# A sum over u moved from identity matmuls on TensorE to fp32 adds on VectorE, and its two PSUM banks given to the pools

## The chip, the cores and the metric

The kernel runs on one core of one Trainium2 chip. The metric is device time in microseconds of one execution, median of several runs; runs marked slow by the harness are left out of every comparison. In the profile PE is TensorE's matmuls, PEld its weight loads, DVE is VectorE, ACT is ScalarE, POOL is GpSimd, SP is the queue that issues loads. The matmuls of this kernel write their results to PSUM, of which its pools hold eight banks; a bank is free again when another engine has read the result out (an "eviction", where it is copied).

## The reference, cut to what matters

It is the forward and backward pass of a speech joint network: two strided convolutions with GELU, then a joint `tanh(fe + ge)` over T=4000 frames and U=8 labels, times `w_o`. The part that the change touches is the gradient of `fe`, which is a sum over the eight labels:

```python
fe = jnp.einsum("btd,de->bte", f, w_f)                 # (2, 4000, 256)
ge = jnp.einsum("bud,de->bue", g, w_g)                 # (2, 8, 256)
j = jnp.tanh(fe[:, :, None, :] + ge[:, None, :, :])    # (2, 4000, 8, 256)
return jnp.einsum("btud,dv->btuv", j, w_o)
# backward of this part, written out:
#   gj   = grad_out @ w_o.T
#   gz   = (1 - j*j) * gj            # per u
#   d_fe = sum over u of gz          # the sum of the title
#   d_ge = sum over t of gz
```

## The kernel before: the parts that matter

The frames are cut into 18 chunks (numbered from 0), nine per batch element: one of 256 frames, seven of 512 and one of 160. The main loop runs three stages side by side, each for another chunk: `stage_a(k+1)` (convolutions, GELU and its derivative), `stage_j(k)` (the joint part, 16 steps) and `stage_de(k-1)` (all remaining gradients). Every step of `stage_j` makes one tile NGZ (the negated gz, one u and one half dt of the 256 features). NGZ goes to a PSUM bank of its own through a matmul with the identity, which adds it to what the bank holds:

```python
    gxp = ctx.enter_context(tc.tile_pool(name="gxp", bufs=2))
    psG = ...bufs=1   # the running gradient of w_o
    psS = ...bufs=1   # sum0, sum1: two banks for the sum over u
    psJ = ...bufs=3   # psj: gj, outputs, transposes of JT
    psA = ...bufs=2   # psa: everything of stage_a and stage_de
    # [...]
    def emit_sum(g_, u, dt, NGZ):
        if u == 0:
            S.setdefault("sum", {})[dt] = psS.tile([P, CW], FP32, name=f"sum{dt}")
        ps = S["sum"][dt]
        nc.tensor.matmul(ps[:, :W], lhsT=ident[:], rhs=NGZ[:, :W], start=(u == 0), stop=(u == U - 1))
        if u == U - 1:
            # [...]
            evac(S["NGFE"][:, dt, :W], ps[:, :W], "act" if dt == 0 else "dve")
    # [...] one step of stage_j: u, dt
                gj = ps_j()
                for kt in range(KT):
                    nc.tensor.matmul(gj[:, :W], lhsT=WOT[:, kt, dt * P:(dt + 1) * P], rhs=GOT[:, j, kt, :W], ...)
                if dt == 0:
                    JSQ = jzp.tile([P, KT, CW], BF16, name="JSQ", bufs=2)
                    nc.vector.tensor_tensor(out=JSQ[:, :, :W], in0=JT[:, j, :, :W], in1=JT[:, j, :, :W], op=ALU.mult)
                NGZ = jzp.tile([P, CW], BF16, name="NGZ")
                nc.vector.scalar_tensor_tensor(out=NGZ[:, :W], in0=JSQ[:, dt, :W], scalar=1.0, in1=gj[:, :W],
                                               op0=ALU.subtract, op1=ALU.mult, accum_out=NGGE_parts[...])
                pend_sum.append((g_, u, dt, NGZ))
                # [...] transposes of JT, their copy JR, the output matmuls, the tanh of the next JT
```

In `stage_a` the product FE is copied from PSUM to SBUF by VectorE in step 7. In `stage_de` each block of the gradient of x is evicted from PSUM as two GX_SB halves, one by ScalarE and one by VectorE, and then stored. GX_SB has two buffers. The tool that builds the kernel chooses the order of the instructions and the waits itself, so an edit can move instructions that it doesn't name.

Of the kernel before, what the change touches and what calls it, by code (L numbers as in the profile page):

```python
# [10 lines left out]
BF16 = mybir.dt.bfloat16  # L11
FP32 = mybir.dt.float32
ALU = mybir.AluOpType
ACT = mybir.ActivationFunctionType
# [7 lines left out]
def kernel(  # L22
# [19 lines left out]
    nc = tc.nc  # L42
    B, T, D = x.shape
    KK = w1.shape[0]
    U = g.shape[1]
# [4 lines left out]
    KT = 2  # L50
    P = 128
# [23 lines left out]
    gop = ctx.enter_context(tc.tile_pool(name="gop", bufs=3))  # L75
    jop = ctx.enter_context(tc.tile_pool(name="jop", bufs=2))
    jrp = ctx.enter_context(tc.tile_pool(name="jrp", bufs=3))
    jzp = ctx.enter_context(tc.tile_pool(name="jzp", bufs=4))
    dep = ctx.enter_context(tc.tile_pool(name="dep", bufs=1))
    dep2 = ctx.enter_context(tc.tile_pool(name="dep2", bufs=2))  # L80
    x5p = ctx.enter_context(tc.tile_pool(name="x5p", bufs=4))
    gxp = ctx.enter_context(tc.tile_pool(name="gxp", bufs=2))
    psG = ctx.enter_context(tc.tile_pool(name="psG", bufs=1, space=bass.MemoryType.PSUM))
    psS = ctx.enter_context(tc.tile_pool(name="psS", bufs=1, space=bass.MemoryType.PSUM))
    psJ = ctx.enter_context(tc.tile_pool(name="psJ", bufs=3, space=bass.MemoryType.PSUM))
    psA = ctx.enter_context(tc.tile_pool(name="psA", bufs=2, space=bass.MemoryType.PSUM))

    def ps_j(dt=FP32):
        return psJ.tile([P, CW if dt == FP32 else 2 * CW], dt, name="psj" if dt == FP32 else "psjb", tag="psj")
# [73 lines left out]
    NGGE_all = accp.tile([P, B, KT, U], FP32, name="NGGE_all")  # L163
    NGGE_parts = accp.tile([P, B, KT, U, NC], FP32, name="NGGE_parts")
    GE = accp.tile([P, B, KT, U], FP32, name="GE")
    GWO_ps = psG.tile([P, KT, V], FP32, name="GWO_ps")

    def make_ge():
# [16 lines left out]
    def evac(out, in_, eng=None):  # L185
        if eng is None:
            eng = "act" if ev_ctr[0] % 2 == 0 else "dve"
            ev_ctr[0] += 1
        if eng == "act":
            nc.scalar.copy(out=out, in_=in_)  # L190
        else:
            nc.vector.tensor_copy(out=out, in_=in_)  # L192
# [50 lines left out]
    def stage_a(g_):  # L243
        b, ci, c0, W = chunks[g_]
        S = st[g_]
        XC = xc_tiles.pop(g_)
        if g_ + 1 < NG:
            xc_tiles[g_ + 1] = load_xc(g_ + 1)
        HTe = htp.tile([P, KT, CW], BF16, name="HTe")
        HTo = htp.tile([P, KT, 2 + CW], BF16, name="HTo")  # L250
        G1e = keep.tile([P, KT, CW], BF16, name="G1e")
        G1o = keep.tile([P, KT, 2 + CW], BF16, name="G1o")
        if ci == 0:
            nc.gpsimd.memset(HTo[:, :, 0:2], 0.0)
            nc.gpsimd.memset(G1o[:, :, 0:2], 0.0)
        else:
            pv = st[g_ - 1]
            pw = chunks[g_ - 1][3]
            nc.gpsimd.tensor_copy(out=HTo[:, :, 1:2], in_=pv["HTo"][:, :, pw + 1:pw + 2])
            nc.gpsimd.tensor_copy(out=G1o[:, :, 1:2], in_=pv["G1o"][:, :, pw + 1:pw + 2])  # L260
        S["HTo"], S["G1e"], S["G1o"] = HTo, G1e, G1o
        mm_o = [(W1[:, i, kt], XC[c][:, kt, 16:16 + W]) for i, c in ((0, 1), (1, 2), (2, 3)) for kt in range(KT)]
        yield from conv_gelu(W, mm_o, HTo[:, :, 2:2 + W], G1o[:, :, 2:2 + W])
        mm_e = [(W1[:, i, kt], XC[c][:, kt, 16 + sh:16 + sh + W])
                for i, c, sh in ((0, 3, -1), (1, 0, 0), (2, 1, 0)) for kt in range(KT)]
        yield from conv_gelu(W, mm_e, HTe[:, :, 0:W], G1e[:, :, 0:W], ps_j if g_ == 0 else None)
        last = c0 + W == MQ
        FT = htp.tile([P, KT, CW], BF16, name="FT")
        G2 = keep.tile([P, KT, CW], BF16, name="G2")
        S["G2"] = G2  # L270
        mm_f = [(W2[:, i, kt], SRC[:, kt, off:off + W])
                for i, SRC, off in ((0, HTo, 1), (2, HTo, 2), (1, HTe, 0)) for kt in range(KT)]
        yield from conv_gelu(W, mm_f, FT[:, :, 0:W], G2[:, :, 0:W])
        S["FE"] = []
        for mt in range(KT):
            ps = ps_a()
            for kt in range(KT):
                nc.tensor.matmul(ps[:, :W], lhsT=WF[:, kt, mt * P:(mt + 1) * P], rhs=FT[:, kt, :W],  # L278
                                 start=(kt == 0), stop=(kt == KT - 1))
            FE = fep.tile([P, CW], FP32, name=f"FE{mt}")  # L280
            evac(FE[:, :W], ps[:, :W], "dve")
            S["FE"].append(FE)
        yield
        HRo = keep.tile([P, NB, D], BF16, name="HRo")
        HRe = keep.tile([P, NB, D], BF16, name="HRe")
        FR = keep.tile([P, NB, D], BF16, name="FR")
        S["HRo"], S["HRe"], S["FR"] = HRo, HRe, FR
        to_rows(HRo, HTo, 1, W + 1 if last else W)
        yield
        to_rows(HRe, HTe, 0, W)  # L290
        yield
        to_rows(FR, FT, 0, W)
        yield
# [20 lines left out]
                                     start=(n == 0), stop=(n == n_gwo - 1))  # L314
                    gwo_cnt[0] = n + 1

    pend_sum, pend_gwo = [], []

    def emit_sum(g_, u, dt, NGZ):
        W = chunks[g_][3]  # L320
        S = st[g_]
        if u == 0:
            S.setdefault("sum", {})[dt] = psS.tile([P, CW], FP32, name=f"sum{dt}")
        ps = S["sum"][dt]
        nc.tensor.matmul(ps[:, :W], lhsT=ident[:], rhs=NGZ[:, :W], start=(u == 0), stop=(u == U - 1))
        if u == U - 1:
            if "NGFE" not in S:
                S["NGFE"] = dep2.tile([P, KT, CW], BF16, name="NGFE")
            evac(S["NGFE"][:, dt, :W], ps[:, :W], "act" if dt == 0 else "dve")

    def stage_j(g_):

# [2 lines left out]
        for up in range(UP):  # L335
# [8 lines left out]
            for step in range(4):  # L344
# [7 lines left out]
                        after(mm, conv_last, sync=False)  # L352
                if dt == 0:
                    JSQ = jzp.tile([P, KT, CW], BF16, name="JSQ", bufs=2)
                    nc.vector.tensor_tensor(out=JSQ[:, :, :W], in0=JT[:, j, :, :W], in1=JT[:, j, :, :W], op=ALU.mult)  # L355
                NGZ = jzp.tile([P, CW], BF16, name="NGZ")
                nc.vector.scalar_tensor_tensor(out=NGZ[:, :W], in0=JSQ[:, dt, :W], scalar=1.0, in1=gj[:, :W],  # L357
                                               op0=ALU.subtract, op1=ALU.mult,
                                               accum_out=NGGE_parts[:, b, dt, u, ci:ci + 1])
                pend_sum.append((g_, u, dt, NGZ))  # L360
                if len(pend_sum) > 2:
                    emit_sum(*pend_sum.pop(0))
                if step % 2 == 0:
                    tbs = [t_ for t_ in nblk[g_] if t_[0] // 2 == step // 2]
                    if tbs:
# [72 lines left out]
    def stage_de(g_):  # L438
# [86 lines left out]
        for bl, m in sblk:  # L525
            GX = gxp.tile([P, 4, D], BF16, name="GX_SB")
            for cp in range(2):
                ps = ps_a()
                for cj in range(2):
                    mms = [(SRC[:, kt, off + bl * P:off + bl * P + m], W1T[:, i, kt, :])  # L530
                           for SRC, off, i in rows4[2 * cp + cj] for kt in range(KT)]
                    for k, (l_, r_) in enumerate(mms):
                        nc.tensor.matmul(ps[:m, cj * D:(cj + 1) * D], lhsT=l_, rhs=r_,  # L533
                                         start=(k == 0), stop=(k == len(mms) - 1))
                evac(GX[:m, 2 * cp:2 * cp + 2].rearrange("p c d -> p (c d)"), ps[:m, :], "act" if cp == 0 else "dve")
                yield
            s0 = c0 + bl * P
            r0, r1 = (1 if s0 == 0 else 0), (m - 1 if s0 + m - 1 == MQ else m)
            dst = out_1[b, 0:1, :]
            flat = GX[:].rearrange("p c d -> p (c d)")  # L540
            if r0 == 1:
                nc.gpsimd.dma_start(out=out_1[b, 0:1, :], in_=GX[0:1, 3, :])
            nc.gpsimd.dma_start(out=bass.AP(tensor=dst.tensor, offset=dst.offset + (4 * (s0 + r0) - 3) * D,
                                            ap=[[4 * D, r1 - r0], [1, 4 * D]]), in_=flat[r0:r1])
            if r1 < m:
                nc.gpsimd.dma_start(out=out_1[b, 4 * MQ - 3:4 * MQ, :].rearrange("(o f) d -> o f d", o=1),
                                    in_=GX[r1:m, 0:3, :])
# [10 lines left out]
    nc.scalar.activation(out=warm_[:, 1, 0:8], in_=warm[:, 0:8], func=ACT.Gelu_apprx_tanh)  # L558
    for _ in range(20):
        nc.tensor.matmul(warm_ps[:, 0:2 * P], lhsT=warm[:, 0:P], rhs=warm, start=True, stop=True)  # L560
    gen = stage_a(0)
    next(gen)
    first_mm, conv_o = marks[0], marks[5]
    nc.sync.dma_start_transpose(out=WOT[:], in_=w_o[:, :])
    st[0]["GOT"], st[0]["GO"] = {0: load_got(0, 0)}, {0: load_gor(0, 0)}
    next(gen)
    next(gen)
    next(gen)
# [57 lines left out]
    for k in range(NG + 1):  # L626
# [14 lines left out]
                for _ in gen:  # L641
                    pass
        if k == NG - 1:
            while pend_sum:
                emit_sum(*pend_sum.pop(0))
            while pend_gwo:
                emit_gwo(*pend_gwo.pop(0))
            gg_out()
            store(out_7, GWO_ps[:])
# [30 lines left out]
```

## Time and profile before

| | before |
|---|---|
| median of 4 runs | 1015.1 us (1007.6 to 1018.6) |
| profiled run | 1005.3 us, clock 0.988 |
| PE, DVE, ACT busy | 966.8, 780.4, 558.6 us |
| a full chunk, mean of ten | 59.96 us |

The "full chunk" is worked out from the trace: the time between NGZ number 16k and number 16(k+1), which is one chunk of `stage_j`, over the ten chunks of 512 frames that have such chunks on both sides as well (k = 2 to 6 and 10 to 14).

The page of the kernel before, its parts 1 and 2 (busy time and share of each engine; then 40 slices of the span, each digit a busy share in tenths):

```profile
span 1005.3 us, 20283 instructions
## 1 busy us (share of the span) xinstructions
PE 966.8 (96%) x8060; PEld 696.6 (69%) x8060; DVE 780.4 (78%) x1733; ACT 558.6 (56%) x983; POOL 211.3 (21%) x402
## 2 busy tenths in 40 slices
PE   5899999999999999999999999999999999999997
...
DVE  3988886959778696868787885958879597877673
ACT  3966674655556464535755664636656455554522
```

TensorE is busy from the second slice to the last but one, and VectorE swings between 5 and 9 with the period of a chunk.

One steady chunk of the kernel before, cut at every fourth NGZ (columns: busy time of each engine with its number of instructions, then clock and DMA):

```profile
core 0: us, PE busy (x) PEld busy (x) DVE busy (x) ACT busy (x) POOL busy (x), PEclk, DMA share, GB/s
162.60:176.20 13.60, 13.50 (x95) 8.19 (x93) 11.05 (x22) 8.45 (x16) 2.82 (x6) 1.00 1.15 210
176.20:192.90 16.70, 16.60 (x132) 10.77 (x130) 16.56 (x36) 10.60 (x17) 1.90 (x4) 1.00 0.80 196
192.90:207.20 14.30, 14.30 (x143) 11.85 (x142) 11.53 (x23) 10.59 (x18) 2.08 (x4) 1.00 0.29 90
207.20:221.70 14.50, 14.45 (x129) 11.66 (x126) 8.71 (x18) 4.67 (x9) 4.65 (x9) 1.00 0.53 162
```

In the second quarter (steps 5 to 8) both PE (16.60 of 16.70 us) and DVE (16.56) look full.

The groups of the kernel before that the change names (busy us, mean ns of one):

```profile
L357 DVE SCALAR_TENSOR_TENSOR NGZ<-JSQ,psj 128x512 bf16<-128x512 bf16 (+2 forms) x288 | 174.2, 611 | 55.3 <-PE psj L349 54.9
L355 DVE TENSOR_TENSOR JSQ<-JT 128x1024 bf16<-128x1024 bf16 (+2 forms) x144 | 87.3, 615 | 2.4
L192 DVE CAST GX_SB<-psa 128x512 bf16<-128x512 f32 x64 | 44.2, 691 | 45.0 <-PE psa L533 33.6
```

The 288 identity matmuls took 58.6 us of TensorE's time from each one's start to the next matmul's start; a full one, 512 columns, takes 216 ns in that sense, although its own record says 379 ns, since matmuls overlap.

The waits of the kernel before that concern GX_SB (total us, times, longest):

```profile
ACT GX_SB L190 <- DMA out_dram<-GX_SB: 37.1, 14, 4.8
DVE GX_SB L192 <- DMA out_dram<-GX_SB: 11.2, 8, 2.3
PE psa L502 <- ACT GX_SB L190: 9.6, 8, 2.2
```

The evictions wait for an older store to leave their buffer, hold their psa bank meanwhile, and TensorE then waits for the bank.

### The profile page before, as it was taken

What the parts mean: (1) busy time and instruction counts of PE and PEld (TensorE: products, weight loads), DVE (VectorE), ACT (ScalarE), POOL (GpSimd) and SP (SyncE); (2) the same over time, 40 slices, a digit from 0 to 9 for tenths busy, and PEclk for the clock granted to TensorE, in tenths of its full rate; (3) what the DMA queues carried; (4) which work ended last, traced back from release to release, by engine and by line L of the source; (5) the groups of instructions that cost most, each with busy time, mean ns of one, the idle gap of its engine ahead of it and who ended that gap; (6) DMA issues with size and microseconds to landing.
All of it is one profiled execution on the core that took longest, in us unless ns stands there. A gap on an engine that the chain in (4) does not pass through costs nothing.

```text
span 1005.3 us, 20283 instructions
## 1 busy us (share of the span) xinstructions
PE 966.8 (96%) x8060; PEld 696.6 (69%) x8060; DVE 780.4 (78%) x1733; ACT 558.6 (56%) x983; POOL 211.3 (21%) x402
## 2 busy tenths in 40 slices
PE   5899999999999999999999999999999999999997
PEld 4567676776767668785765676676867767787873
DVE  3988886959778696868787885958879597877673
ACT  3966674655556464535755664636656455554522
POOL 2122112121111213123231112121121211212230
PEclk7999999999999999999999999999999999999997
DMA  8998848569473774947473847749484684836232
GB/s 168 178 219 207 191 126 180 145 179 196 137 179 107 147 192 148 172 138 197 120 187 103 192 112 179 162 127 220 130 197 110 162 175 130 170 119 168 93 109 61
DMA packets 237919, 156.58 MB, mean 156 GB/s; under 512 B 209504, under 2 KB 213632, under 8 KB 237824
## 3 DMA queue, kind: packets, MB, share of 16 engines
q0 software_dynamic: 29152, 102.69, 34.2%
q1 hardware_dynamic: 206800, 51.68, 31.4%
q8 instruction: 63, 1.03, 0.4%
q10 hardware_dynamic: 1872, 0.92, 0.3%
q14 instruction: 32, 0.26, 0.1%
HBM read 54.44 MB, written 50.34 MB: 104 GB/s over the span
## 4 chain that ended last, share of the span: by engine, by line
PE 80%; ACT 7%; DMA 6%; DVE 5%; SPq 1%; issue 1%; ACTq 0%; DVEq 0%; POOLq 0%
PE psa L502 14%; PE GWO_ps L313 10%; PE psj L387 9%; PE psa L233 9%; PE psj L349 9%; PE psa L533 7%; PE psab L199 6%; PE psjb L371 5%; DMA out_dram<-GX_SB 5%; PE psa L476 3%; ACT JT L300 2%; ACT g_s L216 1%; PE psa L482 1%; DMA GOT<-in_grad_out_dram 1%; ACT OUT_SB L190 1%; PE psa L278 1%
## 5 line engine op out<-in xcount | busy, mean ns | idle before, releaser
L190 ACT CAST OUT_SB<-psj 128x512 bf16<-128x512 f32 (+1 forms) x256 | 150.3, 587 | 165.4 <-PE psj L387 161.2
L357 DVE SCALAR_TENSOR_TENSOR NGZ<-JSQ,psj 128x512 bf16<-128x512 bf16 (+2 forms) x288 | 174.2, 611 | 55.3 <-PE psj L349 54.9
L349 PE MATMUL psj<-GOT,WOT 128*128 128x512 bf16 (+2 forms) x576 | 158.0, 351 | 7.8 <-DMA GOT<-in_grad_out_dram 6.6
L387 PE MATMUL psj<-WO,JT 128*128 128x256 bf16 (+1 forms) x1024 | 162.6, 273 | 0.2
L313 PE MATMUL GWO_ps<-GO_R,JR 128*128 128x256 bf16 (+1 forms) x1024 | 140.6, 273 | 0.0
L210 ACT ACTIVATE g_sq<-psa 128x512 bf16<-128x512 f32 (+2 forms) x106 | 57.7, 544 | 125.1 <-PE psa L233 122.7
L387 PEld LDWEIGHTS <-JT 128*128 128x128 bf16 (+1 forms) x1024 | 93.7, 98 | 38.5 <-issue 3.2
L313 PEld LDWEIGHTS <-JR 128*128 128x128 bf16 (+1 forms) x1024 | 98.5, 98 | 19.2 <-issue 2.3
L129 POOL DMA_DIRECT2D GO_R<-in_grad_out_dram x72 | 52.8, 734 | 268.5 <-PE GWO_ps L313 174.7
L192 DVE COPY JR<-psjb 128x1024 bf16<-128x1024 bf16 (+2 forms) x136 | 88.4, 653 | 10.7 <-PE psjb L371 10.7
L233 PE MATMUL psa<-XC,W_120 128*128 128x512 bf16 (+2 forms) x420 | 92.4, 353 | 1.3 <-DMA XC<-in_x_dram 1.2
L398 POOL DMA_DIRECT2D out_dram<-OUT_SB x72 | 53.4, 742 | 177.8 <-ACT OUT_SB L190 143.3
L355 DVE TENSOR_TENSOR JSQ<-JT 128x1024 bf16<-128x1024 bf16 (+2 forms) x144 | 87.3, 615 | 2.4
L371 PEld LDWEIGHTS <-JT 128*128 128x128 bf16 (+1 forms) x1024 | 69.9, 98 | 27.3 <-issue 0.9
L371 PE MATMUL psjb<-ident,JT 128*128 128x128 bf16 (+1 forms) x1024 | 88.0, 219 | 0.0
L192 DVE CAST GX_SB<-psa 128x512 bf16<-128x512 f32 x64 | 44.2, 691 | 45.0 <-PE psa L533 33.6
L436 DVE TENSOR_TENSOR ACC_GW_148<-ACC_GW_148,psa 128x512 f32<-128x512 f32 x48 | 33.0, 688 | 57.5 <-PE psa L502 57.5
L190 ACT CAST GX_SB<-psa 128x512 bf16<-128x512 f32 x64 | 37.4, 585 | 71.3 <-DMA out_dram<-GX_SB 37.1
L533 PE MATMUL psa<-W1T,GHo 128*128 128x256 bf16 (+1 forms) x384 | 74.1, 275 | 1.2 <-ACT GX_SB L190 1.0
L212 DVE SCALAR_TENSOR_TENSOR g_s<-g_sq,psa 128x512 bf16<-128x512 bf16 (+2 forms) x106 | 65.1, 614 | 12.2 <-ACT HTo L211 11.1
L349 PEld LDWEIGHTS <-WOT 128*128 128x128 bf16 x576 | 54.8, 98 | 28.4 <-DMA WOT<-in_w_o_dram 5.8
L533 PE MATMUL psa<-W1T,GHe 128*128 128x256 bf16 (+1 forms) x384 | 74.0, 275 | 0.1
(616 smaller groups left out, 1886.5 us busy)
## 6 DMA issues: line engine op xcount, KB each, us to landing
GO_R<-in_grad_out_dram POOLq DMA_DIRECT2D x56, 512.0 KB, 4.6
out_dram<-OUT_SB POOLq DMA_DIRECT2D x56, 512.0 KB, 5.4
out_dram<-GX_SB POOLq DMA_DIRECT2D x60, 256.0 KB, 3.2
GOT<-in_grad_out_dram SPq DMA_TRANSPOSE x144, 5.4
GO_R<-in_grad_out_dram POOLq DMA_DIRECT2D x8, 256.0 KB, 4.4
out_dram<-OUT_SB POOLq DMA_DIRECT2D x8, 256.0 KB, 4.5
XC<-in_x_dram SPq DMA_TRANSPOSE x72, 4.7
out_dram<-g_sq SPq DMA_DIRECT2D x9, 128.0 KB, 1.9
```

Source lines behind the costliest of these rows:

```text
L190: nc.scalar.copy(out=out, in_=in_)
L192: nc.vector.tensor_copy(out=out, in_=in_)
L212: nc.vector.scalar_tensor_tensor(out=th, in0=sq, scalar=1.0, in1=ps, op0=ALU.add, op1=ALU.mult)
L233: mm = nc.tensor.matmul(ps[:, :W], lhsT=w[:, mt * P:(mt + 1) * P], rhs=rhs, start=(k == 0), stop=(k == len(mms) - 1))
L313: nc.tensor.matmul(GWO_ps[:, dt, :], lhsT=JR[:m, tb % 2, j, dt * P:(dt + 1) * P], rhs=GO[:m, tb, j, :], start=(n == 0), stop=(n == n_gwo - 1))
L349: mm = nc.tensor.matmul(gj[:, :W], lhsT=WOT[:, kt, dt * P:(dt + 1) * P], rhs=GOT[:, j, kt, :W], start=(kt == 0), stop=(kt == KT - 1))
L355: nc.vector.tensor_tensor(out=JSQ[:, :, :W], in0=JT[:, j, :, :W], in1=JT[:, j, :, :W], op=ALU.mult)
L357: nc.vector.scalar_tensor_tensor(out=NGZ[:, :W], in0=JSQ[:, dt, :W], scalar=1.0, in1=gj[:, :W], op0=ALU.subtract, op1=ALU.mult, accum_out= ...
L371: nc.tensor.transpose(out=tr[:m, o:o + P], in_=JT[:, jj, kt, tb * P:tb * P + m], identity=ident[:])
L387: nc.tensor.matmul(ps[:m, jj * V:(jj + 1) * V], lhsT=JT[:, jj, kt, tb * P:tb * P + m], rhs=WO[:, kt, :], start=(kt == 0), stop=(kt == KT - 1))
L502: nc.tensor.matmul(ps[:, dt * D:(dt + 1) * D], lhsT=lhs(bl, m, dt), rhs=rhs[:m, bl, :], start=(k == 0), stop=(k == n - 1))
L533: nc.tensor.matmul(ps[:m, cj * D:(cj + 1) * D], lhsT=l_, rhs=r_, start=(k == 0), stop=(k == len(mms) - 1))
```

## The change

Its intent: take the identity matmuls off TensorE, pay for the sum with adds on VectorE, and pay for those adds by moving squares and fp32 copies from VectorE to ScalarE. The two banks of the sum go to psj (3 to 4) and psa (2 to 3), and GX_SB gets a third buffer, for which the tiles HRo, HRe and FR (rows of the forward results, kept for the gradients) give up one of three. The core of the diff:

```diff
+    keep2 = ctx.enter_context(tc.tile_pool(name="keep2", bufs=2))        # HRo, HRe, FR (were 3)
-    gxp = ctx.enter_context(tc.tile_pool(name="gxp", bufs=2))
+    gxp = ctx.enter_context(tc.tile_pool(name="gxp", bufs=3))
-    psS = ctx.enter_context(tc.tile_pool(name="psS", bufs=1, ...PSUM))
-    psJ = ctx.enter_context(tc.tile_pool(name="psJ", bufs=3, ...PSUM))
-    psA = ctx.enter_context(tc.tile_pool(name="psA", bufs=2, ...PSUM))
+    psJ = ctx.enter_context(tc.tile_pool(name="psJ", bufs=4, ...PSUM))
+    psA = ctx.enter_context(tc.tile_pool(name="psA", bufs=3, ...PSUM))
+    ZS = accp.tile([P, KT, CW], FP32, name="ZS")
-            evac(FE[:, :W], ps[:, :W], "dve")
+            evac(FE[:, :W], ps[:, :W], "act")
-                    nc.vector.tensor_tensor(out=JSQ[...], in0=JT[...], in1=JT[...], op=ALU.mult)
+                    nc.scalar.activation(out=JSQ[...], in_=JT[...], func=ACT.Square)
-                NGZ = jzp.tile([P, CW], BF16, name="NGZ")
+                first, fin_ = u == 0, u == U - 1
+                NGZ = ZS[:, dt] if first else jzp.tile([P, CW], FP32, name="NGZ", bufs=2)
                 nc.vector.scalar_tensor_tensor(out=NGZ[:, :W], ...)
-                pend_sum.append((g_, u, dt, NGZ))          # -> identity matmul
+                if not first:
+                    nc.vector.tensor_tensor(out=S["NGFE"][:, dt, :W] if fin_ else ZS[:, dt, :W],
+                                            in0=ZS[:, dt, :W], in1=NGZ[:, :W], op=ALU.add)
-                evac(GX[...], ps[:m, :], "act" if cp == 0 else "dve")
+                evac(GX[...], ps[:m, :], "act")
 # [...] at the start, the loads of WOT and of the first GOT and GO are issued before those of the second chunk's x
```

More of the change, by code (lines that the diff above doesn't have):

```diff
@@ L81 @@
     x5p = ctx.enter_context(tc.tile_pool(name="x5p", bufs=4))
-    gxp = ctx.enter_context(tc.tile_pool(name="gxp", bufs=2))
+    gxp = ctx.enter_context(tc.tile_pool(name="gxp", bufs=3))
     psG = ctx.enter_context(tc.tile_pool(name="psG", bufs=1, space=bass.MemoryType.PSUM))
-    psS = ctx.enter_context(tc.tile_pool(name="psS", bufs=1, space=bass.MemoryType.PSUM))
-    psJ = ctx.enter_context(tc.tile_pool(name="psJ", bufs=3, space=bass.MemoryType.PSUM))
-    psA = ctx.enter_context(tc.tile_pool(name="psA", bufs=2, space=bass.MemoryType.PSUM))
+    psJ = ctx.enter_context(tc.tile_pool(name="psJ", bufs=4, space=bass.MemoryType.PSUM))
+    psA = ctx.enter_context(tc.tile_pool(name="psA", bufs=3, space=bass.MemoryType.PSUM))
     def ps_j(dt=FP32):
@@ L280, in stage_a @@
             FE = fep.tile([P, CW], FP32, name=f"FE{mt}")
-            evac(FE[:, :W], ps[:, :W], "dve")
+            evac(FE[:, :W], ps[:, :W], "act")
             S["FE"].append(FE)
         yield
-        HRo = keep.tile([P, NB, D], BF16, name="HRo")
-        HRe = keep.tile([P, NB, D], BF16, name="HRe")
-        FR = keep.tile([P, NB, D], BF16, name="FR")
+        HRo = keep2.tile([P, NB, D], BF16, name="HRo")
+        HRe = keep2.tile([P, NB, D], BF16, name="HRe")
+        FR = keep2.tile([P, NB, D], BF16, name="FR")
         S["HRo"], S["HRe"], S["FR"] = HRo, HRe, FR
@@ L315, in emit_gwo @@
                     gwo_cnt[0] = n + 1
-    pend_sum, pend_gwo = [], []
-    def emit_sum(g_, u, dt, NGZ):
-        W = chunks[g_][3]
-        S = st[g_]
-        if u == 0:
-            S.setdefault("sum", {})[dt] = psS.tile([P, CW], FP32, name=f"sum{dt}")
-        ps = S["sum"][dt]
-        nc.tensor.matmul(ps[:, :W], lhsT=ident[:], rhs=NGZ[:, :W], start=(u == 0), stop=(u == U - 1))
-        if u == U - 1:
-            if "NGFE" not in S:
-                S["NGFE"] = dep2.tile([P, KT, CW], BF16, name="NGFE")
-            evac(S["NGFE"][:, dt, :W], ps[:, :W], "act" if dt == 0 else "dve")
+    pend_gwo = []
     def stage_j(g_):
@@ L354, in stage_j @@
                     JSQ = jzp.tile([P, KT, CW], BF16, name="JSQ", bufs=2)
-                    nc.vector.tensor_tensor(out=JSQ[:, :, :W], in0=JT[:, j, :, :W], in1=JT[:, j, :, :W], op=ALU.mult)
-                NGZ = jzp.tile([P, CW], BF16, name="NGZ")
+                    if True:
+                        nc.scalar.activation(out=JSQ[:, :, :W], in_=JT[:, j, :, :W], func=ACT.Square)
+                    else:
+                        nc.vector.tensor_tensor(out=JSQ[:, :, :W], in0=JT[:, j, :, :W], in1=JT[:, j, :, :W],
+                                                op=ALU.mult)
+                first, fin_ = u == 0, u == U - 1
+                NGZ = ZS[:, dt] if first else jzp.tile([P, CW], FP32, name="NGZ", bufs=2)
                 nc.vector.scalar_tensor_tensor(out=NGZ[:, :W], in0=JSQ[:, dt, :W], scalar=1.0, in1=gj[:, :W],
@@ L359, in stage_j @@
                                                accum_out=NGGE_parts[:, b, dt, u, ci:ci + 1])
-                pend_sum.append((g_, u, dt, NGZ))
-                if len(pend_sum) > 2:
-                    emit_sum(*pend_sum.pop(0))
+                if fin_ and dt == 0:
+                    S["NGFE"] = dep2.tile([P, KT, CW], BF16, name="NGFE")
+                if not first:
+                    nc.vector.tensor_tensor(out=S["NGFE"][:, dt, :W] if fin_ else ZS[:, dt, :W], in0=ZS[:, dt, :W],
+                                            in1=NGZ[:, :W], op=ALU.add)
                 if step % 2 == 0:
@@ L534, in stage_de @@
                                          start=(k == 0), stop=(k == len(mms) - 1))
-                evac(GX[:m, 2 * cp:2 * cp + 2].rearrange("p c d -> p (c d)"), ps[:m, :], "act" if cp == 0 else "dve")
+                evac(GX[:m, 2 * cp:2 * cp + 2].rearrange("p c d -> p (c d)"), ps[:m, :], "act")
                 yield
@@ L560 @@
         nc.tensor.matmul(warm_ps[:, 0:2 * P], lhsT=warm[:, 0:P], rhs=warm, start=True, stop=True)
+    nc.sync.dma_start_transpose(out=WOT[:], in_=w_o[:, :])
+    st[0]["GOT"], st[0]["GO"] = {0: load_got(0, 0)}, {0: load_gor(0, 0)}
     gen = stage_a(0)
@@ L563 @@
     first_mm, conv_o = marks[0], marks[5]
-    nc.sync.dma_start_transpose(out=WOT[:], in_=w_o[:, :])
-    st[0]["GOT"], st[0]["GO"] = {0: load_got(0, 0)}, {0: load_gor(0, 0)}
     next(gen)
@@ L643 @@
         if k == NG - 1:
-            while pend_sum:
-                emit_sum(*pend_sum.pop(0))
             while pend_gwo:
```

## The prediction

> **What bounds the kernel now.** TensorE. The page gives PE busy 966.8 of 1005.3 us (96%) at clock 0.988, and the chain that ended last is 80% PE. "Busy" flatters it: costing the 8060 matmuls at the trace's back-to-back starts (216 ns for 512 columns, 109 for 256) they need about 916 us (an estimate); 84 us are waits, start and tail. DVE is busy 780 us (78%), ACT 559 (56%). Averages hide stages. Cutting a steady chunk (59 to 61 us, 16 steps) at every fourth NGZ operation of the instruction records, at start-to-start costs: steps 1-4 13.6 us, PE 0.98, DVE 0.78, ACT 0.58; steps 5-8 16.7 us, PE 0.96, **DVE 0.99**, ACT 0.60; steps 9-12 14.3 us, PE 0.97, DVE 0.76, ACT 0.69; steps 13-16 14.2 to 16.5 us, PE down to 0.86, DVE 0.5, ACT 0.26. The last varies as GX_SB waits for its older store (37 us in the list of waits; 4.6% of the chain).
>
> **Removed.** 288 identity matmuls: 58.6 us of PE. On DVE: 144 squares JSQ (686 ns, 600 start to start; 76 us), 36 FE copies (19 us), 64 GX casts (38 us), half the NGFE evictions (5 us).
>
> **Added.** DVE: 252 fp32 adds. The Trainium skill ("VectorE: DVE Perf Modes", tier table and errata section) keeps fp32 tensor_tensor in 1x and gives (N+151)/0.96 = 691 ns at N=512. The trace's fp32 accumulator adds (one PSUM operand) agree: 686 to 688 ns, 600 start to start. So 196 x 0.60 plus the narrow ones = 133 us: DVE comes out level in sum, plus bubbles: JSQ and the NGZ that reads it now start 744 ns apart, not 600; an add reads what was just written, so where nothing is interleaved it costs 0.14 us more: 10 to 20 us. ACT: 144 squares (its 128x1024 tanh takes 1067 ns, 957 start to start: 121 us), FE (15), GX (30): ACT rises to about 75% busy.
>
> **On the critical path.** PE work per full chunk falls 16 x 0.216 = 3.5 us. In steps 5-8 DVE stays at 16.5 us (lost: 2 squares, 2 FE copies; gained: 4 adds), so DVE sets that quarter, and steps 1-4 rise to DVE 11.8 of 12.8 us: the first half of the chunk gains about 1 us of its 1.7. Steps 9-12 gain nearly 0.9 us, with ACT near 0.93. Steps 13-16 gain 0.9, and the third GX_SB buffer and third psa bank should take away most GX store waits (10 to 15 us in all). WOT and the first GOT loaded ahead of the second chunk's x shorten the 5.8 us wait for GOT at the start by 2 to 4 us. Two HRo/HRe/FR buffers instead of three make their evictions wait for the older chunk's weight-gradient matmuls: 0 to 8 us. Sum: -55 us.
>
> **Predicted: 957 us**, 935 to 985 (8 in 10). Faster by over 2%: 0.87; within 2%: 0.11; slower: 0.02.
>
> **What would show it.** 7772 matmuls, PE busy near 910 us; DVE within 20 us of 780; ACT near 740; adds near 690 ns, NGZ near 680; GX_SB's store waits mostly gone; steps 5-8 near 16 us with DVE at 0.98 or more; new waits of gj matmuls (psj) for NGZ, or of NGZ for the ACT square.
>
> **What would make it wrong.** Adds dearer than 600 ns; ACT's in-order queue delaying squares, NGZ and its PSUM bank; the two-buffer row tiles blocking; the instruction order changing more than the diff shows; DMA (66% share now) stalling a faster kernel.

## The result, and the profile after

| | before | after |
|---|---|---|
| median | 1015.1 us | 949.5 us |
| fast runs | 1007.6 to 1018.6 (4) | 945.5 to 950.2 (3) |
| profiled run | 1005.3 us | 947.0 us |
| full chunk, mean of ten | 59.96 us | 56.27 us |

The ratio is 0.935, with a 95% interval of 0.927 to 0.943: faster. A fourth run after, of 974 us, was marked slow. Ratios here are the mean time of one kernel's fast runs over the mean of the other's fast runs in the same rounds, so they are not quite the ratio of the medians quoted beside them.

The page of the changed kernel, parts 1 and 2:

```profile
span 947.0 us, 19927 instructions
## 1 busy us (share of the span) xinstructions
PE 911.3 (96%) x7772; PEld 670.1 (71%) x7772; DVE 756.0 (80%) x1723; ACT 710.1 (75%) x1209; POOL 212.7 (22%) x402
## 2 busy tenths in 40 slices
PE   7888999999999999999999999999999999999997
...
DVE  4969895978869697877778796978969687887673
ACT  5979887777968778675878787787878779685642
```

PE has 288 matmuls fewer and is busy 55.5 us less, DVE is about level, ACT has 151.5 us more. PE's share is 96% as before.

A steady chunk of the changed kernel, cut in the same way:

```profile
158.70:174.40 15.70, 15.36 (x112) 9.47 (x110) 12.53 (x26) 13.66 (x22) 3.29 (x7) 1.00 1.11 260
174.40:191.10 16.70, 16.41 (x142) 11.68 (x141) 16.70 (x35) 12.96 (x22) 2.18 (x4) 1.00 0.67 140
191.10:201.70 10.60, 10.18 (x105) 8.50 (x103) 8.70 (x19) 9.60 (x16) 2.07 (x3) 1.00 0.35 100
201.70:215.00 13.30, 13.30 (x126) 11.24 (x124) 8.45 (x17) 7.58 (x14) 4.16 (x8) 1.00 0.55 172
```

The second quarter still lasts 16.70 us with DVE at 16.70 (near 16 us was predicted); but the third lost 3.7 us, and the first gained 2.1. The whole chunk is shorter by 3.7 us.

The groups of the changed kernel that answer to those of before:

```profile
L351 DVE SCALAR_TENSOR_TENSOR NGZ<-JSQ,psj 128x512 f32<-128x512 bf16 (+2 forms) x252 | 152.1, 609 | 53.6 <-PE psj L338 33.5
L345 ACT ACTIVATE JSQ<-JT 128x1024 bf16<-128x1024 bf16 (+2 forms) x144 | 137.7, 956 | 16.5 <-DVE NGZ L351 16.0
L357 DVE TENSOR_TENSOR ZS<-ZS,NGZ 128x512 f32<-128x512 f32 (+2 forms) x216 | 132.1, 612 | 1.3
L191 ACT CAST GX_SB<-psa 128x512 bf16<-128x512 f32 (+1 forms) x128 | 73.3, 591 | 4.8 <-PE psa L529 4.2
```

An fp32 result makes NGZ no dearer (the full ones last 679 ns, 681 before). A full add lasts 683 ns (mean) and the next operation starts 602 ns after it (median). The bubble that the prediction feared (an add that reads what was just written starts late) is there, but rare: of the 252 adds 52 stand directly behind the NGZ that they read, 42 of them full ones, and these start 0.71 to 0.73 us after it, where an operation that doesn't read NGZ starts 0.61 us after it (median). That makes about 5 us in all (an estimate from these counts); before the other adds at least one more operation is interleaved. No wait of GX_SB for its own store appears in the list of waits any more.

Where the 58.3 us between the two profiled runs lie, by the same cuts (us of the span):

| stretch | before | after | difference |
|---|---|---|---|
| to the first NGZ | 25.3 | 21.3 | -4.0 |
| chunks 0 and 1 | 78.5 | 81.3 | +2.8 |
| ten full chunks | 599.6 | 562.7 | -36.9 |
| the other six chunks and the tail | 301.9 | 281.7 | -20.2 |

The first NGZ comes 4.0 us earlier, and the next two chunks give 2.8 us of that back.

### The profile page after: what moved, and what is told of

Same layout as the page of the kernel before. It is cut to its first block, busy times and chain, and to the rows that moved or that the text cites. A ratio compares the mean times of both kernels' runs of the same rounds, so it can differ in the third digit from the quotient of the medians.

```text
span 947.0 us, 19927 instructions
## 1 busy us (share of the span) xinstructions
PE 911.3 (96%) x7772; PEld 670.1 (71%) x7772; DVE 756.0 (80%) x1723; ACT 710.1 (75%) x1209; POOL 212.7 (22%) x402
## 3 DMA queue, kind: packets, MB, share of 16 engines
q0 software_dynamic: 29152, 102.69, 36.9%
## 4 chain that ended last, share of the span: by engine, by line
PE 57%; ACT 27%; DVE 10%; DMA 2%; SPq 2%; issue 2%; DVEq 0%; ACTq 0%
PE psa L498 12%; PE psa L529 9%; ACT JT L301 8%; PE psj L383 8%; PE psj L338 6%; PE GWO_ps L314 6%; ACT JSQ L345 5%; PE psa L234 5%; PE psjb L367 4%; ACT OUT_SB L191 3%; PE psab L200 3%; PE psa L472 3%; ACT g_sq L211 2%; DVE g_s L213 2%; DVE GF L463 2%
## 5 line engine op out<-in xcount | busy, mean ns | idle before, releaser
L351 DVE SCALAR_TENSOR_TENSOR NGZ<-JSQ,psj 128x512 f32<-128x512 bf16 (+2 forms) x252 | 152.1, 609 | 53.6 <-PE psj L338 33.5
L301 ACT ACTIVATE JT<-FE,GE 128x512 bf16<-128x512 f32 (+2 forms) x288 | 183.0, 684 | 0.0
L383 PE MATMUL psj<-WO,JT 128*128 128x256 bf16 (+1 forms) x1024 | 157.5, 274 | 1.3 <-DVE JR L193 1.3
L345 ACT ACTIVATE JSQ<-JT 128x1024 bf16<-128x1024 bf16 (+2 forms) x144 | 137.7, 956 | 16.5 <-DVE NGZ L351 16.0
L357 DVE TENSOR_TENSOR ZS<-ZS,NGZ 128x512 f32<-128x512 f32 (+2 forms) x216 | 132.1, 612 | 1.3
L432 DVE TENSOR_TENSOR ACC_GW<-ACC_GW,psa 128x512 f32<-128x512 f32 x96 | 65.3, 683 | 60.5 <-PE psa L498 60.5
L234 PEld LDWEIGHTS <-W 128*128 128x128 bf16 x648 | 61.9, 98 | 47.1 <-issue 4.6
L234 PE MATMUL psa<-XC,W 128*128 128x512 bf16 (+2 forms) x420 | 92.7, 353 | 1.3 <-DMA XC<-in_x_dram 0.7
L498 PEld LDWEIGHTS <-X 128*128 128x128 bf16 (+1 forms) x768 | 75.0, 98 | 14.0 <-issue 0.6
L191 ACT CAST GX_SB<-psa 128x512 bf16<-128x512 f32 (+1 forms) x128 | 73.3, 591 | 4.8 <-PE psa L529 4.2
```

The lines of the kernel that those rows point to most:

```text
L191: nc.scalar.copy(out=out, in_=in_)
L234: mm = nc.tensor.matmul(ps[:, :W], lhsT=w[:, mt * P:(mt + 1) * P], rhs=rhs, start=(k == 0), stop=(k == len(mms) - 1))
L301: nc.scalar.activation(out=JT[:, j, mt, :W], in_=st[g_]["FE"][mt][:, :W], func=ACT.Tanh, bias=GE[:, b, mt, 2 * up + j:2 * up + j + 1], sca ...
L345: nc.scalar.activation(out=JSQ[:, :, :W], in_=JT[:, j, :, :W], func=ACT.Square)
L357: nc.vector.tensor_tensor(out=S["NGFE"][:, dt, :W] if fin_ else ZS[:, dt, :W], in0=ZS[:, dt, :W], in1=NGZ[:, :W], op=ALU.add)
L383: nc.tensor.matmul(ps[:m, jj * V:(jj + 1) * V], lhsT=JT[:, jj, kt, tb * P:tb * P + m], rhs=WO[:, kt, :], start=(kt == 0), stop=(kt == KT - 1))
```

## The experiments

Two readings stood against each other. The first, that of the prediction: TensorE's removed work is the gain, and VectorE caps it, since VectorE sets the pace of steps 5 to 8. The second: VectorE's fullness there is only a queue running behind, TensorE sets the pace throughout, and what decides is whether TensorE finds free PSUM banks. A third thing to settle was how much each part brings. Each run was timed in three rounds against the kernel before on its chip (medians of before: 1013.0 to 1015.2 us). "Chunk" is the full chunk as above, and "NGZ 33" the time at which chunk 2 begins.

| run | median us | ratio to before | chunk us | NGZ 33 at us |
|---|---|---|---|---|
| before | 1015 | 1 | 59.96 | 103.8 |
| b_gx3 | 1002.3 | 0.991 | 59.31 | 109.1 |
| b_moves | 1019.1 | 1.007 | 60.86 | 108.5 |
| the changed kernel | 949.5 | 0.935 | 56.27 | 102.6 |
| a_fe_dve | 962.9 | 0.947 | 57.10 | 102.6 |
| a_gx_dve | 949.7 | 0.935 | 56.27 | 103.5 |
| a_sq_dve | 959.5 | 0.949 | 56.07 | 113.4 |
| a_bf16 | 944.1 | 0.927 | 55.78 | 105.1 |
| a_noadd (wrong) | 939.7 | 0.926 | 55.98 | 98.3 |
| a_fe_dve_noadd (wrong) | 943.1 | 0.933 | 55.52 | 106.5 |
| a_banks_before | 989.0 | 0.978 | 58.57 | 105.1 |
| a_psa2 | 981.0 | 0.968 | 57.71 | 107.2 |
| a_psj3 | 955.3 | 0.943 | 56.59 | 106.3 |
| a_bf16_psa4 | 933.0 | 0.918 | 55.08 | 103.4 |

The intervals of the ratios are about plus or minus 0.007, some 7 us, and the changed kernel was not timed again beside its variants; so a difference of 5 to 10 us between two variants rests more on the chunk column, where most full chunks of one run agree within 0.1 us. The last column comes from one profiled execution and also depends on when loads land: TensorE's waits for GOT sum to between 1.4 us (a_fe_dve) and 12.1 us (a_sq_dve) over these runs. All results but the two marked ones were correct.

### FE back on VectorE, and half of GX back on VectorE

```diff
 # a_fe_dve
-            evac(FE[:, :W], ps[:, :W], "act")
+            evac(FE[:, :W], ps[:, :W], "dve")
 # a_gx_dve
-                evac(GX[...], ps[:m, :], "act")
+                evac(GX[...], ps[:m, :], "act" if cp == 0 else "dve")
```

> The changed kernel with its 36 FE evictions back on VectorE (19 us of DVE work, all in steps 5-8 of a chunk). Stage theory (VectorE sets the pace of steps 5-8, where it is 1.00 occupied): each full chunk grows by 2 x 0.6 us, so about +12 to +18 us: 961 to 968 us. Rival (TensorE alone sets the pace, VectorE at 80% has room): within 4 us of the changed kernel, 945 to 953 us.

> The changed kernel with half of the GX evictions back on VectorE (64 casts, 38 us of DVE work, twice that of the FE run, but in steps 9-16 where VectorE is 0.8 and 0.6 occupied). Stage theory: within 5 us of the changed kernel (945 to 954 us). If instead VectorE's total counted, it would cost about twice what the FE run costs, 25 us or more.

Measured: FE costs 13 us (962.9 against 949.5) for 19 us of VectorE work; GX costs nothing (949.7) for twice as much. So it matters where in the chunk VectorE's work lies, and not only how much there is. But the two runs don't yet say that VectorE sets the pace of steps 5 to 8. VectorE in the run with FE on VectorE, and then in the changed kernel, around the same place of the same chunk (start, length, line, operation):

```profile
188.40 0.68 DVE L223 TENSOR_TENSOR G<-g_om,g_s 128x1024 bf16<-128x1024 bf16 x1
189.00 1.28 DVE L193 COPY FE<-psa 128x512 f32<-128x512 f32 x2
190.20 0.67 DVE L432 TENSOR_TENSOR ACC_GWF<-ACC_GWF,psa 128x512 f32<-128x512 f32 x1
190.79 0.67 DVE L351 SCALAR_TENSOR_TENSOR NGZ<-JSQ,psj 128x512 f32<-128x512 bf16 x1
```

```profile
187.51 0.68 DVE L223 TENSOR_TENSOR G<-g_om,g_s 128x1024 bf16<-128x1024 bf16 x1
188.11 0.68 DVE L432 TENSOR_TENSOR ACC_GWF<-ACC_GWF,psa 128x512 f32<-128x512 f32 x1
188.71 0.67 DVE L351 SCALAR_TENSOR_TENSOR NGZ<-JSQ,psj 128x512 f32<-128x512 bf16 x1
```

The two FE copies put 1.2 us ahead of two operations that each set a PSUM bank free: the add ACC_GWF a psa bank, the NGZ a psj bank. But TensorE's waits begin earlier, and they point to the banks that the copies themselves hold. The matmuls that made FE, and the next that needs a psa bank, with FE on VectorE (in brackets the idle time before and what ended it):

```profile
184.57 0.59 PE L279 MATMUL psa<-FT,WF 128*128 128x512 bf16 x2
187.20 1.03 PE L498 MATMUL psa<-NFR,FR 128*128 128x256 bf16 x8 [0.71 <-ACT GFR L191]
```

In the changed kernel:

```profile
183.68 0.59 PE L279 MATMUL psa<-FT,WF 128*128 128x512 bf16 x2
184.26 1.08 ACT L191 COPY FE<-psa 128x512 f32<-128x512 f32 x2
185.35 1.04 PE L498 MATMUL psa<-NFR,FR 128*128 128x256 bf16 x8
```

On VectorE the FE copies wait in a queue without a gap, and end 5.3 us after their matmuls (counted from the last matmul's start plus 216 ns; chunks 3 to 6), against 1.2 to 1.4 us on ScalarE. Meanwhile two of the three psa banks are taken. Costed as in "The banks" below, TensorE's waits in steps 5 to 8 rise from 0.79 to 1.74 us, 0.87 us of them before these NFR matmuls, 0.46 us behind VectorE's late copy JR, which frees a psj bank.

### FE on VectorE without the adds

```diff
 # a_fe_dve_noadd: a_fe_dve, and
-                if not first:
+                if fin_:
                     nc.vector.tensor_tensor(out=..., in0=ZS[:, dt, :W], in1=NGZ[:, :W], op=ALU.add)
```

> Wrong on purpose (only the last add of each sum is kept), with the FE evictions on VectorE: the FE run (13 us slower) without the adds. Theory that FE on VectorE costs only because VectorE's queue has a backlog in steps 5-8 there, which delays the evictions behind it: without the adds it costs under 5 us, 937 to 945 us against 939.7 of the run without adds. If FE on VectorE costs by itself, whatever the load: 950 us or more.

Measured: 943.1 us, 3.4 us more than the run without adds and without this edit (939.7, below). So most of the 13 us go when the adds go, as the backlog theory expected: the steady chunk isn't longer with FE on VectorE (55.52 against 55.98 us); what is lost lies before chunk 2 (106.5 against 98.3 us). The trace doesn't show that the queue is empty, though: the FE copies still start 3.1 us or more after their matmuls. Why they then cost nothing in the steady chunk is not shown.

### The adds made cheaper, and left out

```diff
 # a_bf16
-    ZS = accp.tile([P, KT, CW], FP32, name="ZS")
+    ZS = accp.tile([P, KT, CW], BF16, name="ZS")
-                NGZ = ZS[:, dt] if first else jzp.tile([P, CW], FP32, name="NGZ", bufs=2)
+                NGZ = ZS[:, dt] if first else jzp.tile([P, CW], BF16, name="NGZ", bufs=4)
 # a_noadd
-                if not first:
+                if fin_:
```

> The changed kernel with ZS and NGZ in bf16[...]: add 330 ns start to start instead of 600 (414 ns instead of 683 in the record), VectorE busy about 66 us less. Stage theory: steps 5-8 fall from 16.7 to about 15.6 us, whole kernel 8 to 18 us faster, 931 to 941 us. Rival (VectorE not binding): no gain, 945 to 951 us. The gradients are rounded more often, so the comparison with the reference may suffer.

> Wrong on purpose: of the seven adds per sum only the last is kept (216 of 252 adds gone), nothing else changed. This is the upper bound of any cheaper sum. Stage theory: steps 5-8 become bound by TensorE (about 15.3 us), steps 1-4 too; 12 to 30 us faster, 920 to 937 us. Rival (adds lie under TensorE's work): within 4 us of the changed kernel.

Measured: 944.1 and 939.7 us, 5 and 10 us faster than the changed kernel. Both lie between the two ranges, just outside what the prediction's reading expected. (a_bf16 also gives NGZ four buffers instead of two; that was not run apart.) Without six of seven adds the second quarter falls to 15.2 us, but the third rises from 10.6 to 12.7 us, and the chunk falls only from 56.27 to 55.98 us. The largest part of the 9.9 us between the two profiled runs lies before chunk 2, which begins at 98.3 instead of 102.6 us. So the six adds in seven cost about 0.3 us per steady chunk, not the 0.7 us that the prediction withheld.

### Only the moves to ScalarE

```diff
 # b_moves: the kernel before, with
-                    nc.vector.tensor_tensor(out=JSQ[...], in0=JT[...], in1=JT[...], op=ALU.mult)
+                    nc.scalar.activation(out=JSQ[...], in_=JT[...], func=ACT.Square)
-            evac(FE[:, :W], ps[:, :W], "dve")
+            evac(FE[:, :W], ps[:, :W], "act")
-                evac(GX[...], ps[:m, :], "act" if cp == 0 else "dve")
+                evac(GX[...], ps[:m, :], "act")
```

> The kernel before with only the moves to ScalarE (squares, FE, GX evictions); the sum stays on TensorE and the banks and buffers stay as before. VectorE busy falls by about 130 us to 650, ScalarE rises to about 730. My theory: what is worth most is the 58.6 us of TensorE work, so this alone gains little: steps 5-8 fall to TensorE's 16 us, 0 to 15 us faster, 1000 to 1015 us against 1015. Rival (the moves are the gain and VectorE was the bound): 30 us or more faster.

Measured: 1019.1 us, ratio 1.007 (1.000 to 1.014): no gain, if anything a small loss. The page of this run, part 1:

```profile
PE 974.0 (96%) x8060; PEld 697.5 (68%) x8060; DVE 647.4 (63%) x1489; ACT 719.7 (71%) x1227; POOL 212.0 (21%) x402
```

VectorE is relieved of 133 us, and its second quarter does shrink, from 16.7 to 15.1 us; the third grows from 14.3 to 16.8 (columns as above):

```profile
182.00:197.10 15.10, 14.67 (x109) 8.91 (x106) 14.16 (x32) 11.74 (x19) 1.27 (x4) 1.00 0.69 176
197.10:213.90 16.80, 16.55 (x165) 13.57 (x165) 9.09 (x19) 14.57 (x23) 2.69 (x4) 1.00 0.33 97
```

By itself this run leaves a rival: it also loads ScalarE with 161 us, and a new wait there could hide what VectorE's relief gave. TensorE's own records settle it. Costed as in "The banks" below, TensorE waited 0.64 of the 16.7 us of steps 5 to 8 in the kernel before, 0.30 of them directly behind VectorE, and 0.79 of 16.7 us in the changed kernel, 0.16 of them directly behind VectorE (means of chunks 3 to 6). VectorE did not set the pace of steps 5 to 8. The cuts are made at VectorE's own operations. A quarter shows when VectorE gets to an NGZ, and when VectorE is late in one quarter it catches up in the next, while TensorE goes on as long as it has banks. The sum over the chunk is what counts.

### The squares back on VectorE

```diff
 # a_sq_dve
-                        nc.scalar.activation(out=JSQ[...], in_=JT[...], func=ACT.Square)
+                        nc.vector.tensor_tensor(out=JSQ[...], in0=JT[...], in1=JT[...], op=ALU.mult)
```

> The changed kernel with the squares back on VectorE (76 us of work). VectorE would be needed for about 800 us start to start, 0.6 us more in each of 8 pairs of steps; steps 1-8 bound by VectorE at about 31 us instead of 32.3 total as they stand plus 2.4: stage theory +25 to +45 us, 975 to 995 us. If VectorE's average share counted (88% of 950): within 10 us.

Measured: 959.5 us, 10 us slower; the expectation of 25 to 45 us, made on the prediction's reading, was far off. The steady chunk is not longer at all (56.07 us), although its VectorE is busy all through steps 5 to 12. The loss is in the start: chunk 2 begins at 113.4 instead of 102.6 us. So the largest of the moves to ScalarE pays only in the first two chunks. There, TensorE's longest wait is for a load of GOT; in this run and in the changed kernel (total us, times, longest):

```profile
PE psj L338 <- DMA GOT<-in_grad_out_dram: 12.1, 2, 11.5
PE psj L338 <- DMA GOT<-in_grad_out_dram: 5.2, 2, 4.6
```

That is 6.9 of the 10.8 us. VectorE is not full in chunk 0 of this run (busy 29.8 of 42.0 us), only in chunk 1 (47.3 of 49.6). Why the load lands later was not tested, so it is not shown that the squares' place as such is worth 10 us.

### The third GX_SB buffer alone

```diff
 # b_gx3: the kernel before, with
-    gxp = ctx.enter_context(tc.tile_pool(name="gxp", bufs=2))
+    gxp = ctx.enter_context(tc.tile_pool(name="gxp", bufs=3))
+    keep2 = ...bufs=2        # and HRo, HRe, FR from keep2: without this SBUF is too small
```

> The kernel before with the third GX_SB buffer alone (paid for with two instead of three buffers of HRo, HRe and FR, as in the change). Theory: the waits of ScalarE for the older GX_SB store (37 us in the list) go, and with them most of the 11.8 us of TensorE stalls before the X matmuls: 8 to 14 us faster, 1001 to 1007 against 1015. Rival (store waits are off the critical path): within 3 us.

Measured: 1002.3 us against 1013.0, ratio 0.991 (0.984 to 0.998). All full chunks now last 59.3 us, where they lasted 58.8 to 61.2 before, and the waits of ScalarE for the store shrink from 37.1 to 4.8 us. The price of two instead of three row tiles is inside this number and was not measured by itself.

### The banks

```diff
 # a_banks_before: both pools as before, two banks empty
-    psJ = ...bufs=4   psA = ...bufs=3
+    psJ = ...bufs=3   psA = ...bufs=2
 # a_psa2: psJ 4, psA 2, one bank empty        # a_psj3: psJ 3, psA 3, one bank empty
```

> The changed kernel with the pools at their old size (psj 3, psa 2), so that the two freed banks stay empty. Theory: the banks are a small part; with ScalarE and VectorE both fuller the two banks cushion them: 5 to 20 us slower than the changed kernel, 955 to 970 us, TensorE waits before gj and psa matmuls up. If the banks were the main gain: 990 us or more. If they were idle: within 3 us.

Measured: 989.0 us, 39 us slower than the changed kernel: far more than the 5 to 20 us expected. This run has all the work of the changed kernel on the same engines and differs in two empty banks (and in the order that the building tool made of it). Its page, part 1:

```profile
PE 939.5 (95%) x7772; PEld 670.6 (68%) x7772; DVE 759.9 (77%) x1723; ACT 707.3 (72%) x1209; POOL 216.0 (22%) x402
```

Beside the changed kernel, the same 7772 matmuls are "busy" 939.5 instead of 911.3 us: PE's busy time contains short waits, since a matmul's record lasts longer than the next one's distance. The records allow a better account. Costing each matmul at its back-to-back pace (216, 109 and 56 ns for 512, 256 and 128 columns) and taking the rest of the time as waits, per full chunk over four chunks (3 to 6) in which no matmul record is missing:

| per chunk, us | length | matmuls at pace | rest: waits |
|---|---|---|---|
| before | 59.65 | 57.54 | 2.1 |
| b_gx3 | 59.31 | 57.54 | 1.8 |
| b_moves | 60.64 | 57.54 | 3.1 |
| changed kernel | 56.29 | 54.09 | 2.2 |
| a_banks_before | 58.54 | 54.09 | 4.45 |

So removing the identity matmuls gives 3.45 us per chunk. Against the kernel before nearly all of it arrives, with the third GX_SB buffer's 0.65 us (59.96 to 59.31) beside it; against b_gx3, which has that buffer too, 3.0 us arrive with the banks and 0.8 without. Without the banks 2.25 us turn into waits: those before matmuls that write psa rise from 2.2 to 3.2 us, those before matmuls that write psj from nothing to 1.2. Going from b_gx3 to this run, that is with the sum, the squares, FE and GX moved and the first loads reordered but the pools as they were, brought 13 us; the banks brought the other 39. Of the 39.4 us between the two profiled runs 23 lie in the ten full chunks, the rest at the start, at the change of batch element and at the end. What two more banks would be worth with the sum still on TensorE can't be run: all eight are in use there.

> The changed kernel with psa at its old two banks, psj at four, one bank empty. Together the two banks are worth 39 us. The waits that the run with both taken away adds lie mostly before matmuls that write psa (psab<-GF, psa<-W1T, psa<-GFR). Theory that psa is the scarcer pool: 20 to 30 us slower than the changed kernel, 970 to 980 us. If psj is: within 10 us.

> The changed kernel with psj at its old three banks, psa at three, one bank empty. Theory that psa is the scarcer pool: 5 to 15 us slower than the changed kernel, 955 to 965 us, with waits before gj (psj<-GOT,WOT). If psj is the scarcer: 970 us or more. If each bank alone is nearly enough, both runs stay within 10 us and only the pair costs 39.

Measured: the third psa bank is worth 31.5 us (981.0), the fourth psj bank 6 us (955.3); together that is about the 39 of the pair. psa is the scarce pool, although the waits with both banks taken away were split about evenly between matmuls of the two pools: where a wait shows is not always where the bank is missing.

### A version that beats both

```diff
 # a_bf16_psa4: a_bf16, and
-    psJ = ...bufs=4   psA = ...bufs=3
+    psJ = ...bufs=3   psA = ...bufs=4
```

> Search for a version that beats both kernels: the sum in bf16 (944 us alone) and one bank moved from psj to psa (3 and 4). The third psa bank was worth 31 us and the fourth psj bank 6 us. If the waits that are left before the matmuls that write psa are for banks, the fourth psa bank gives 5 to 12 us and the lost psj bank takes less now that VectorE is freer: 932 to 942 us. If they are for data (GHo, GF and NGFE just computed), the bank gives nothing: 944 to 952 us.

Measured: 933.0 us, ratio 0.918 (0.911 to 0.926); three fast runs of 930.2 to 935.0, one slow of 951. It is 1.8% faster than the changed kernel by the two ratios. The same banks with the fp32 sum were not run, so how its gain divides between the two edits is known only for bf16 alone (5 us).

## Why the prediction was right

The time (957 predicted, 949.5 measured, range 935 to 985) and the class were right. Point by point:

- **TensorE bounds the kernel; 58.6 us of its work go.** Right: 7772 matmuls, busy 911.3 us (near 910 predicted), and the full chunk lost its 3.45 us of matmuls. (The 84 us of waits, start and tail should have been 89: 1005.3 less 916.)
- **VectorE comes out level.** Nearly right: 780.4 to 756.0 us, 4 us outside the stated 20. The bubbles, which I put at 10 to 20 us, came to about 5, since only 52 adds stand directly behind their NGZ. The add's length, which I took from the Trainium skill ("VectorE: DVE Perf Modes", errata section, 691 ns at 512) and from the fp32 accumulator adds of the trace, was right: 683 ns.
- **ScalarE rises to 75%.** Right: 75%, 710.1 us. The 740 us in my list of signs was too high; it disagreed with the 166 us added (121, 15 and 30) that I had worked out in the same text. A new wait, which I had listed as a risk, came with it: VectorE's NGZ waited 17.0 us, in ten places, until a GX_SB copy on ScalarE had ended.
- **"DVE sets that quarter", so the first half of the chunk gains little.** This step failed in its reasoning, though the sign to look for came true: steps 5 to 8 lasted 16.70 us with VectorE full. TensorE waited only 0.79 us in them, 0.16 of that directly behind VectorE. Removing 133 us of VectorE work from the kernel before made it no faster (b_moves), and removing six adds in seven changed the steady chunk by 0.3 us. VectorE's backlog cost time where a copy in it held two psa banks (FE, 13 us), and otherwise was caught up. The prediction had the sign against it in its own numbers: PE at 0.96 in that quarter.
- **The third GX_SB buffer and the third psa bank together 10 to 15 us.** The buffer alone is about 9 to 11 us in the kernel before. The psa bank was mis-sized: it is worth 31.5 us in the changed kernel. I had treated the banks as a small extra; they are the condition for the main gain. With the old pools the change brings 2.2% instead of 6.5%, the 0.9% of the GX_SB buffer included.
- **WOT and GOT first: 2 to 4 us.** The first NGZ came 4.0 us earlier, but 2.8 us of it were given back in the next two chunks. The part was not run alone.
- **Two buffers for HRo, HRe and FR: 0 to 8 us lost.** Not measured by itself; inside b_gx3.

By the medians the gain was 65.6 us, 10 us more than the 55 predicted; between the two profiled runs it was 58.3, since the profiled run before is the fastest of its four. What I withheld for VectorE's supposed cap, 0.7 us in each chunk, would come to about 11 us over 8000 frames (15.6 full chunks), but it is not the missing piece: the prediction's own terms give 2.9 to 3.8 us per full chunk (1.0, 0.9 and 0.9, plus 0.6 to 1.0 for the GX_SB buffer and the psa bank, less 0 to 0.5 for the row tiles), and 3.69 were measured. So the closeness is in part luck: a cap that wasn't there was charged, other waits of 0.4 us per chunk came in its place (59.31 of b_gx3 less 3.45 would be 55.86, and 56.27 were measured), and that two banks fewer would have taken most of the gain was not foreseen.

The chain of waits of the changed kernel, by engine, names what has come nearer:

```profile
PE 57%; ACT 27%; DVE 10%; DMA 2%; SPq 2%; issue 2%; DVEq 0%; ACTq 0%
```

Before, it was PE 80%, ACT 7%. ScalarE now stands in it for a quarter of the span, and any further load on it should be weighed first.

## What to carry to other kernels

When work leaves the engine that sets the pace, ask whether the buffers that feed and drain that engine let it run closer: here the moved sum, with the moves that pay for it, was worth 13 us on the old pools and 52 with its two PSUM banks put to use, and a bank for the one pool was worth five times a bank for the other. Don't read from a full stretch of one engine, marked by its own operations, that it sets the pace: take work off it in one run and see whether the whole period shrinks, and count how long the other engine really waits there. When a busy engine gets more work, look at what that work holds while it stands in the queue, and at what stands behind it, since 19 us of copies cost 13 us where they kept two banks for 5.3 us, and 38 us of copies elsewhere cost nothing.

## What the Trainium skill lacked or had wrong

- "VectorE: DVE Perf Modes", errata section, gives two formulas for a VectorE operation and says that 58 + FD cycles under-predicts the duration while (N+151)/0.96 is exact. Both are right for different things: at 512 fp32 elements the record lasts 683 ns (the second gives 691), but back to back the operations start 602 ns apart (the first gives 594). For VectorE's load the row that this section rejects was the better one here; the section doesn't say so, though "Perfetto Trace Analysis", section "Optimizing Scalar/DVE Operations", does tell engine-busy time from profiled latency.
- "Perfetto Trace Analysis", section "Matmul Optimizations", says to use all eight PSUM banks but gives neither a size nor a way to divide them. Here two idle banks cost 39 us of 949, one psa bank 31.5 us and one psj bank 6 us.
- "Perfetto Trace Analysis", section "Identifying the Most-Contended Engine", says that matmul busy time is no good measure of the distance to roofline. The runs agree and add why it misleads in a comparison: 7772 matmuls were busy 911.3 us in one run and 939.5 us in another that differs in two banks, at 96% and 95% of the span; weight loads were busy 670 us in both.
- "ScalarE: Activation LUTs", rules for kernel authors, sends multiplications to VectorE. The square of 1024 bf16 elements took 1066 ns on ScalarE and 686 ns on VectorE, as the page would have it, and still the kernel was 10 us faster with it on ScalarE, all of it in the first two chunks, where most of the difference is a longer wait for a load; in the steady chunks (56.27 against 56.07 us) the place made next to no difference. So the duration of the one operation, on which the rule rests, did not decide here.
- No page warns that cutting a trace at one engine's own operations shows where that engine is, not what the others wait for: quarters of 16.7 and 14.3 us became 15.1 and 16.8 us when VectorE was relieved, in a chunk that got no shorter.
